# Sixteen partitions of the first five output-weight rows go in loads of 5, 5, 3 and 3 partitions

## The chip, the core and the metric

The kernel runs on one core of one Trainium2 chip. The metric is the time of one execution on the device, in microseconds (us). The times named "before" are of the kernel without the change.

## What is computed

A decode step with one new token for two batch rows. Half A is attention over a key and value cache of 16384 positions, 32 heads of 128; half B is a small mixer network; a gate adds them up.

```python
q = (x @ wq).reshape(B, Sq, H, Dh)                      # B=2, Sq=1, H=32, Dh=128, D=1024
scores = einsum("bhqd,bhkd->bhqk", q, k_cache) * Dh**-0.5
o = einsum("bhqk,bhkd->bhqd", softmax(scores), v_cache)
a = o.reshape(B, Sq, H * Dh) @ wo                       # wo: 4096 x 1024
b = x1 + gelu(layernorm(x1) @ w3) @ w4                  # x1 = x + shifted gelu(...) @ w2
out = g * a + (1 - g) * b                               # g = sigmoid(sum(x * gate_w))
```

The two caches are 537 MB of the 570 MB that the kernel reads. The output weights `wo` are 8 MB and are used last.

## The kernel before

All large loads are issued by SyncE (SP) into one ring of five slots in SBUF (`ring`), each of 32 KB in each of 128 partitions. A planner (`queue_load`, `pump`, `release`) keeps one list of loads in the order of use; a load is issued when its slots have been released by the matmuls that read them. First come `wq`, `w2`, `w3` and `w4`, then 32 rounds of a key load `k` and a value load `v` of 8 MB each, and at the end `wo` in two halves: ("wo", 0) into slot 2 and ("wo", 1) into slot 3.

Each partition holds 32 rows of `wo` (row r of partition p is row 32p + r of the matrix, 2 KB long). Half 0 is rows 0 to 15, and before the change it is one load of 128 partitions by 32 KB, made by the helper `runs` and issued on L335. Half 1 is rows 16 to 31; it comes in six pieces (`wo_runs[1]`) of 8, 4, 2, and then by columns 2, 1 and 1 rows, each with a semaphore of its own (`dtl0` to `dtl5`). The first three pieces are issued on L335, the last three, made by `cols_of`, on L341.

A round is: VectorE transposes blocks of the keys in place (L677), TensorE multiplies them by q (L683), a softmax follows (L693 to L710), TensorE multiplies by the values (L719), and the result goes to `OT_sb` (L728 to L733). After the last round `do_aproj` does the output projection: a transpose and a regrouping of `OT_sb` (L740 to L749), then for each row of `wo` four matmuls of 256 columns, each into its own quarter of the PSUM partitions (L766). Half 0 takes 64 of them, behind one wait. For half 1 the matmuls of the first two column quarters are on L766 (32 of them), and those of the other two are split into four of 128 columns per row (L778, 64 of them); each piece waits for its own semaphore. The chain ends with four copies out of PSUM (L804 to L808) and three stores (L806, L809).

Of the kernel before, what the change touches and what calls it, by code (L numbers as in the profile page):

```python
# [120 lines left out]
def build_kernel(nc, A_x, A_k, A_v, A_wq, A_wo, B_w1, B_w2, B_w3, B_w4, gate_w, out, dbg=None):  # L121
    dbg = dbg or {}
    B, Sq, D = A_x.shape
# [4 lines left out]
    P = 128  # L128
# [25 lines left out]
    RS = SLOT // D  # L154
# [6 lines left out]
               [(RS, RS // 2, *full), (RS + RS // 2, RS // 4, *full), (RO - RS // 4, RS // 8, *full),  # L161
                (RO - 2, 2, *lo), (RO - 2, 1, *hi_), (RO - 1, 1, *hi_)]]
    assert all(sum(n * qn for _, n, _, qn in runs) == RS * NQ for runs in wo_runs)
    DQ = D // NQ
    PR = 32 * (NQ - 1) + 2
    assert HQ == 2 and DQ <= 512 and HD == 8 * 512 and F % 8 == 0 and F <= 8 * 512 and P % (2 * NQ) == 0

    with ExitStack() as st:
# [3 lines left out]
        ring = sb("ring", [P, NRS, SLOT], BF16)  # L172
# [32 lines left out]
        OT4_sb = sb("OT4_sb", [P, RO, B], BF16)  # L205
        xrow = sb("xrow", [P, DQ], BF16)
        bgrow = sb("bgrow", [P, DQ], F32)
        orow = sb("orow", [P, DQ], BF16)
        lrow = sb("lrow", [2, 2 * DQ], BF16)
        m24 = sb("m24", [P, 2, NQ], F32)  # L210
# [21 lines left out]
        sem = lambda n: st.enter_context(nc.semaphore(n))  # L232
        esems = {e: sem("e_" + e) for e in ENGS}
        s_ring = [sem(f"dr{i}") for i in range(NRS)]
# [3 lines left out]
        s_out = [sem(f"dout{i}") for i in range(2)]  # L238
        s_fin = [sem(f"dfin{i}") for i in range(2)]
        s_xr = sem("dxr")  # L240
        s_tail = [sem(f"dtl{i}") for i in range(len(wo_runs[1]))]
        pl = _Plan(esems)

        def bank_bf(i):
            return banks[i].bitcast(BF16)
# [47 lines left out]
        dma_done = {}  # L293
# [13 lines left out]
        def pump():  # L307
            while dma_q and (dma_q[0][3] or all(i in slot_free for i in dma_q[0][2])):
                key, fns, slots, more = dma_q.pop(0)
                waits = () if more else sum((slot_free.pop(i) for i in slots), ())  # L310
                slot_of[key] = slots[0]
                slots_of[key] = slots
                for k, fn in enumerate(fns):
                    dsem = s_ring[slots[0]] if len(fns) == 1 else s_tail[k]
                    dyn = key[0] in ("k", "v") and key[1] >= B
                    if dyn and key == ("k", B):
                        pl.mark["sp"] = len(pl.ops["sp"])
                    one = (lambda e, i, fn=fn, idx=slots[0]: fn(e, idx, i)) if dyn else (lambda e, fn=fn, idx=slots[0]: fn(e, idx))
                    dma_done[key] = dma_done[key, k] = pl.dma("sp", one, dsem, waits=waits if k == 0 else (), dyn=dyn)

        def release(key, ev, slots=None):
            for idx in slots or slots_of[key]:
                assert idx not in slot_free
                slot_free[idx] = tuple(ev) if isinstance(ev, (tuple, list)) else (ev,)
            pump()
# [2 lines left out]
            assert key in dma_done, f"load {key} not yet issued in program order (would deadlock)"  # L328
            return dma_done[key]

        def runs(Wt, width, r0, rn, base=0):
            def fn(e, idx):
                src = Wt.rearrange("(p r) n -> p (r n)", p=P)[:, r0 * width:(r0 + rn) * width]
                flat = ring[:, idx:, :].rearrange("p s m -> p (s m)")
                return e.dma_start(flat[:, (r0 - base) * width:(r0 - base + rn) * width], src)  # L335
            return fn

        def cols_of(Wt, width, r0, rn, c0, cn, base):
            def fn(e, idx):
                dst = ring[:, idx, :].rearrange("p (r n) -> p r n", n=width)[:, r0 - base:r0 - base + rn, c0:c0 + cn]  # L340
                return e.dma_start(dst, Wt.rearrange("(p r) n -> p r n", p=P)[:, r0:r0 + rn, c0:c0 + cn])  # L341
            return fn

        wloads = {}
# [3 lines left out]
        for hi in range(2):  # L348
            wloads[("wo", hi)] = [runs(A_wo, D, r0, rn, hi * RS) if qn == NQ else cols_of(A_wo, D, r0, rn, q0 * DQ, qn * DQ, hi * RS)
                                  for r0, rn, q0, qn in wo_runs[hi]]  # L350
        wloads[("w2", 0)] = [runs(B_w2, D, 0, NBD)]

        w_slots = {"wq": (0, 1), "w2": (2,), "w3": (3, 4), "w4": (0, 1)}
# [27 lines left out]
        evd = {}  # L381
# [185 lines left out]
        key = ("w2", 0)  # L567
        put([row_stage(key, list(range(NBD)), 0, NBD, lambda kc: shT_bf[:, kc, :], "const", last=True), hs_columns], key)
        put([st_x1, ln_a(x1T_f[:, :, :], "x1", st2_ps, "xn2"), ln_b(st2_ps, "xn2", None)])
        key = ("w3", 0)  # L570
        put([w3_rows(kl) for kl in range(NBD)] + [w3_columns], key)
        put([gelu2])
        key = ("w4", 0)
# [16 lines left out]
        for pi in range(2):  # L590
            queue_load(("wo", pi), wloads[("wo", pi)], ((2, 3)[pi],))
        pump()

        def xcols(row, b_n, nb):
# [19 lines left out]
        key = ("wq", 0)  # L614
# [122 lines left out]
        def do_aproj():  # L737
            or_ps = bank_bf(7)[0:G, 256:256 + P]
            o4_ps = banks[3][:, 0:B * RO].rearrange("p (b r) -> p b r", b=B)
            e1 = pl.add("pe", lambda e: e.transpose(or_ps, OT_sb[:, :], ident[:, :]), waits=(ev_OT,), sig=True)  # L740
            e2 = pl.add("dve", lambda e: e.tensor_copy(OR_sb[:, :], or_ps), waits=(e1,), sig=True)  # L741
            ev = None
            for b in range(B):
                for dq in range(QO):
                    ev = pl.add("pe", lambda e, b=b, dq=dq: e.matmul(  # L745
                        o4_ps[:, b, :], lhsT=esel[:, b, :, dq], rhs=OR_sb[:, RO * dq:RO * (dq + 1)], start=(dq == 0), stop=(dq == QO - 1),
                        skip_group_check=True), waits=(e2, ev_const) if b + dq == 0 else (), sig=(b == B - 1 and dq == QO - 1))
            ev_half = [None, None]
            ev_o4 = pl.add("dve", lambda e: e.tensor_copy(OT4_sb[:, :, :].rearrange("p r b -> p b r"), o4_ps), waits=(ev,), sig=True)  # L749
            QC = DQ // 2  # L750
            ev_q2 = None
            for hi in range(2):
                key = ("wo", hi)
                wt = ring[:, slot_of[key], :].rearrange("p (r n) -> p r n", r=RS)
                for k, (r0, rn, q0, qn) in enumerate(wo_runs[hi]):
                    w = (dma_done[key, k], ev_o4, evd["bg"])
                    late = hi == 1
                    if late and ev_q2 is None:
                        for t in range(2):
                            ev_q2 = pl.add("dve", lambda e, t=t: e.tensor_copy(  # L760
                                q2_ps[64 * t:64 * t + 34, 0:QC], rows2_ps[64:98, QC * t:QC * (t + 1)]), waits=(ev_half[1],), sig=True)
                    wide = range(q0, min(q0 + qn, HQ) if late else q0 + qn)
                    for r in range(r0, r0 + rn):
                        for qd in wide:
                            ps = half(qd)
                            ev = pl.add("pe", lambda e, r=r, qd=qd, wt=wt, ps=ps: e.matmul(  # L766
                                ps[32 * qd:32 * qd + 2, 0:DQ], lhsT=OT4_sb[:, r, :], rhs=wt[:, r % RS, qd * DQ:(qd + 1) * DQ],
                                start=False, stop=True, tile_position=(0, 32 * qd), skip_group_check=True), waits=w,
                                sig=(qd == wide[-1]))
                            w = ()  # L770
                            ev_half[qd // HQ] = ev
                    if not late or q0 + qn == HQ:
                        continue
                    w = w + (ev_q2,)
                    for r in range(r0, r0 + rn):
                        for qd in range(NQ):
                            c = D // 2 + DQ * (qd % 2) + QC * (qd // 2)
                            ev_half[1] = pl.add("pe", lambda e, r=r, qd=qd, wt=wt, c=c: e.matmul(  # L778
                                q2_ps[32 * qd:32 * qd + 2, 0:QC], lhsT=OT4_sb[:, r, :], rhs=wt[:, r % RS, c:c + QC],
                                start=False, stop=True, tile_position=(0, 32 * qd), skip_group_check=True), waits=w,  # L780
                                sig=(qd == NQ - 1))
                            w = ()
            return ev_half
# [3 lines left out]
        for n in range(NPR):  # L787
# [3 lines left out]
            for k in range(0, NU, TC):  # L791
                ev_t = do_T(n, us[k])
                for t in range(TC):
                    w = () if t else (ev_t,) if k else (ev_t, ev_z) + pro_ev
# [51 lines left out]
def bass_gated_mix__mha_block_cached__mixer_s_mlp__decode_kernel(  # L846
    nc: bass.Bass,
    A_x: bass.AP,
    A_k_cache: bass.AP,
    A_v_cache: bass.AP,  # L850
    A_wq: bass.AP,
    A_wo: bass.AP,
    B_x: bass.AP,
    B_w1: bass.AP,
    B_w2: bass.AP,
    B_w3: bass.AP,
    B_w4: bass.AP,
    gate_w: bass.AP,
    out: bass.AP,
):  # L860
    build_kernel(nc, A_x, A_k_cache, A_v_cache, A_wq, A_wo, B_w1, B_w2, B_w3, B_w4, gate_w, out)
# [28 lines left out]
```

## Time and profile before

| what | value |
|---|---|
| median of 3 runs | 1324.05 us (1323.98 to 1324.16) |
| profiled execution, its time | 1324.2 us |
| profiled execution, span of its instructions | 1322.9 us |
| outside the span | 1.3 us |
| TensorE busy, VectorE busy | 59%, 50% of the span |
| read from HBM | 570.44 MB, 431 GB/s over the span |

The profile is of one execution, so sums are made against its 1324.2 us. It lies 0.15 us over the median of the runs shown. A time in the trace counts from the start of the span.

### The profile page before, as it was taken

How to read it: one execution, taken by the hardware profiler on the slowest of the kernel's cores; microseconds unless marked ns; L12 is line 12 of the kernel's file. 1: busy time of each engine (PE TensorE's matmuls, PEld its weight loads, DVE VectorE, ACT ScalarE, POOL GpSimd, SP SyncE). 2: the span in 40 equal slices, each digit the busy share in tenths (PEclk: the TensorE clock that was granted, in tenths of full speed). 3: DMA queues.
4: the chain of work that ended last, by engine and by line, in shares of the span. 5: the costliest groups of instructions: out<-in, count | busy, mean ns of one | idle time of the engine just before them, and what ended most of it. 6: DMA issues, size and time to landing. Idle time of an engine off the chain costs nothing. (4 is left out here: it accounts for less than half of the span.)

```text
span 1322.9 us, 12021 instructions
## 1 busy us (share of the span) xinstructions
PE 785.9 (59%) x4951; PEld 322.6 (24%) x4951; DVE 667.8 (50%) x541; ACT 46.4 (4%) x101; POOL 20.8 (2%) x96
## 2 busy tenths in 40 slices
PE   2345557655556765555676555567655556756557
PEld 1212222222222222222232222223222222322223
DVE  2264445655444665544466554446655445665444
ACT  0000000000000000000000000000000000000000
POOL 2000000000000000000000000000000000000000
PEclk9576788777678877767877776787777678777768
DMA  9999999999999999999999999999999999999998
GB/s 423 430 425 436 434 438 428 434 442 424 434 442 424 434 442 424 434 442 424 434 442 424 434 442 424 434 442 424 434 442 424 434 442 424 436 440 424 436 440 362
DMA packets 11114, 570.56 MB, mean 431 GB/s; under 512 B 1233, under 2 KB 1759, under 8 KB 1890
## 3 DMA queue, kind: packets, MB, share of 16 engines
q1 hardware_dynamic: 11080, 570.43, 99.7%
q8 instruction: 6, 0.10, 0.0%
q10 hardware_dynamic: 26, 0.01, 0.0%
q14 instruction: 2, 0.02, 0.0%
HBM read 570.44 MB, written 0.00 MB: 431 GB/s over the span
## 5 line engine op out<-in xcount | busy, mean ns | idle before, releaser
L683 PE MATMUL ps<-ring,Z 128*128 128x512 bf16 x2048 | 533.2, 418 | 377.3 <-DVE ring L677 376.3
L677 DVE STREAM_TRANSPOSE ring<-ring 128x2048 f32<-128x2048 f32 x256 | 565.2, 2275 | 264.8 <-DMA ring<-in_A_k_cache_dram 264.8
L683 PEld LDWEIGHTS ps<-ring,Z 128*128 128x128 bf16 x2048 | 203.4, 104 | 694.4 <-issue 457.1
L719 PE MATMUL ps<-ring,PT_sb 128*32 128x512 bf16 x2048 | 178.8, 526 | 4.3 <-DVE recip L710 3.9
L733 DVE SCALAR_TENSOR_TENSOR OT_sb<-ps,gT,recip 128x2 f32 x32 | 7.0, 220 | 214.3 <-PE ps L730 214.3
L719 PEld LDWEIGHTS ps<-ring,PT_sb 128*32 128x32 bf16 x2048 | 69.8, 127 | 99.4 <-issue 83.4
L704 ACT ACTIVATE P_sb<-ps,negm 128x512 bf16<-128x512 f32 x32 | 22.0, 687 | 1000.0 <-DVE negm L702 1000.0
L693 DVE TENSOR_REDUCE rA<-ps 128x1 f32<-128x512 f32 x32 | 22.1, 692 | 64.2 <-PE ps L683 64.2
L708 PE MATMUL ps<-rowsum,hsel 128*128 128x1 f32 x128 | 24.2, 293 | 38.0 <-ACT P_sb L704 38.0
L706 DVE STREAM_TRANSPOSE PT_sb<-P_sb 128x512 bf16<-128x512 bf16 x32 | 22.8, 712 | 27.1 <-ACT P_sb L704 27.1
L708 PEld LDWEIGHTS ps<-rowsum,hsel 128*128 128x128 f32 x128 | 21.5, 238 | 40.7 <-ACT P_sb L704 40.7
L663 POOL TENSOR_TENSOR Z<-q_f,mask 128x8 bf16<-128x8 f32 x64 | 12.3, 228 | 1210.2 <-PE ps L683 1210.2
L695 PE MATMUL ps<-ident,rmax_bf 128*1 128x128 bf16 x32 | 6.9, 217 | 33.1 <-DVE rmax_bf L694 33.1
L728 ACT ACTIVATE acc_sb<-ps 128x512 bf16<-128x512 f32 x32 | 19.1, 597 | 209.8 <-PE ps L719 209.8
L730 PE MATMUL ps<-dsel,acc_sb 128*128 128x2 bf16 x128 | 8.1, 167 | 22.6 <-ACT acc_sb L728 22.6
L621 PE MATMUL ps<-ring,xT_bf 128*2 128x512 bf16 x64 | 5.2, 494 | 16.4 <-DMA ring<-in_A_wq_dram 16.4
L730 PEld LDWEIGHTS ps<-dsel,acc_sb 128*128 128x128 bf16 x128 | 5.3, 96 | 38.3 <-ACT acc_sb L728 38.3
L695 PEld LDWEIGHTS ps<-ident,rmax_bf 128*1 128x1 bf16 x32 | 2.5, 79 | 48.9 <-DVE rmax_bf L694 48.9
L696 DVE TENSOR_REDUCE m_sb<-ps 1x2 bf16<-1x128 bf16 x32 | 8.9, 279 | 9.9 <-PE ps L695 9.9
L702 DVE TENSOR_SCALAR negm<-ps,cAB 128x1 f32<-128x1 f32 x32 | 8.9, 278 | 9.2 <-PE ps L699 9.2
L699 PE MATMUL ps<-m_sb,ones_bf 1*64 1x1 bf16 x64 | 6.1, 186 | 11.9 <-DVE m_sb L696 11.9
L520 PE MATMUL ps<-ring,GT_bf 128*2 128x256 bf16 x112 | 5.2, 372 | 6.8 <-DMA ring<-in_B_w_dram 6.8
(113 smaller groups left out, 93.6 us busy)
## 6 DMA issues: line engine op xcount, KB each, us to landing
ring<-in_B_w_dram SPq DMA_DIRECT2D x2, 7168.0 KB, 39.1
ring<-in_A_wq_dram SPq DMA_DIRECT2D x1, 7168.0 KB, 21.3
ring<-in_A_wo_dram SPq DMA_DIRECT2D x1, 4096.0 KB, 37.5
ring<-in_B_w_dram SPq DMA_DIRECT2D x1, 2048.0 KB, 25.5
ring<-in_A_wo_dram SPq DMA_DIRECT2D x1, 2048.0 KB, 22.1
ring<-in_A_wq_dram SPq DMA_DIRECT2D x1, 1024.0 KB, 4.6
ring<-in_A_wo_dram SPq DMA_DIRECT2D x1, 1024.0 KB, 24.3
ring<-in_A_k_cache_dram SPq DMA_DIRECT2D x32, 26.7
```

Of the source, the lines that this page charges most:

```text
L663: return e.tensor_tensor(Z[:, :, ZO:ZO + P].rearrange("p t (i c) -> p t i c", c=32)[:, :, 2 * hp:2 * hp + 2, hp], q4_f[:, :, col].broadcas ...
L677: return pl.add("dve", lambda e: e.transpose(ap, ap), waits=(arrived(("k", n)),), sig=True)
L683: ev = pl.add("pe", lambda e, bp=bp: e.matmul(S_ps[:, 0:NCOL], lhsT=Z[:, bp, ZO - 2 * u:ZO - 2 * u + P], rhs=kv[:, :, bp // 2, :, bp % 2], ...
L693: e1 = pl.add("dve", lambda e: e.tensor_reduce(rA[:, :], S_ps[:, 0:NCOL], axis=AX.X, op=ALU.max), waits=(ev_S[n],), sig=True)
L695: e3 = pl.add("pe", lambda e: e.transpose(mt_ps, rmax_bf[:, :], ident[:, :]), waits=(e2,), sig=True)
L696: e4 = pl.add("dve", lambda e: e.tensor_reduce(m_sb[0:1, :], mt_ps.rearrange("o (h p) -> o h p", h=HP), axis=AX.X, op=ALU.max), waits=(e3, ...
L704: e7 = pl.add("act", lambda e: e.activation(P_sb[:, :], S_ps[:, 0:NCOL], ACT.Exp, bias=negm[:, 0:1], scale=scale, accum_out=rowsum[:, 0:1] ...
L706: e8 = pl.add("dve", lambda e: e.transpose(PT_sb[:, :], P_sb[:, :]), waits=(e7,), sig=True)
L708: e9 = pl.add("pe", lambda e, hp=hp: e.matmul(l_ps[:, hp:hp + 1], lhsT=hsel[:, hp, :], rhs=rowsum[:, 0:1], start=True, stop=True, skip_gro ...
L719: ev = pl.add("pe", lambda e, jj=jj, cg=cg: e.matmul(acc_ps[32 * cg:32 * cg + 32, 0:512], lhsT=PT_sb[:, 32 * jj:32 * jj + 32], rhs=vv[:, 4 ...
L728: e1 = pl.add("act", lambda e: e.activation(acc_sb[:, :], acc_ps[:, 0:512], ACT.Copy), waits=(ev_pv,), sig=True)
L730: e2 = pl.add("pe", lambda e, w=w: e.matmul(oT_ps, lhsT=acc_sb[:, w * P:(w + 1) * P], rhs=dsel[:, w, :], start=(w == 0), stop=(w == 3)), w ...
```

## The change

Half 0 of `wo`, rows 0 to 15, is no longer one load. Rows 0 to 4 of partitions 0 to 111 are one load, rows 5 to 15 of all 128 partitions are a second, and rows 0 to 4 of partitions 112 to 127 come in four more loads of 5, 5, 3 and 3 partitions. The bytes are the same and they land in the same places. The first two loads have a semaphore each (`dw0`, `dw1`), the four short ones share the third (`dw2`). All six are issued where the one was, and all wait for the same slot. The first matmul of half 0 waits for all three semaphores.

```diff
+    ER = 5
+    e_parts = (5, 5, 3, 3)
+    EP = P - sum(e_parts)
...
+        s_w0 = [sem(f"dw{i}") for i in range(3)]
...
-                    dsem = s_ring[slots[0]] if len(fns) == 1 else s_tail[k]
+                    dsem = s_ring[slots[0]] if len(fns) == 1 else s_w0[min(k, 2)] if key == ("wo", 0) else s_tail[k]
...
-        def runs(Wt, width, r0, rn, base=0):
+        def runs(Wt, width, r0, rn, base=0, p0=0, pn=P):
             def fn(e, idx):
-                src = Wt.rearrange("(p r) n -> p (r n)", p=P)[:, r0 * width:(r0 + rn) * width]
-                flat = ring[:, idx:, :].rearrange("p s m -> p (s m)")
+                src = Wt.rearrange("(p r) n -> p (r n)", p=P)[p0:p0 + pn, r0 * width:(r0 + rn) * width]
+                flat = ring[p0:p0 + pn, idx:, :].rearrange("p s m -> p (s m)")
...
+        wloads[("wo", 0)] = [runs(A_wo, D, 0, ER, 0, 0, EP), runs(A_wo, D, ER, RS - ER, 0)]
+        wloads[("wo", 0)] += [runs(A_wo, D, 0, ER, 0, EP + sum(e_parts[:j]), k) for j, k in enumerate(e_parts)]
...
-                    w = (dma_done[key, k], ev_o4, evd["bg"])
+                    w = (dma_done[key, k], ev_o4, evd["bg"]) + ((dma_done[key, 1], dma_done[key, 1 + len(e_parts)]) if hi == 0 else ())
```

On SP, behind the loop over the rounds, this is what stood after the last value load (partitions by elements of 2 bytes):

```order
L100 COMPARE_AND_BRANCH
L335 DMA ring<-in_A_wo_dram 128x16384
L335 DMA ring<-in_A_wo_dram 128x8192 [waits e_pe]
L335 DMA ring<-in_A_wo_dram 128x4096
L335 DMA ring<-in_A_wo_dram 128x2048
```

And this is what stands there now:

```order
L100 COMPARE_AND_BRANCH
L340 DMA ring<-in_A_wo_dram 112x5120
L340 DMA ring<-in_A_wo_dram 128x11264
L340 DMA ring<-in_A_wo_dram 5x5120 x2
L340 DMA ring<-in_A_wo_dram 3x5120 x2
L340 DMA ring<-in_A_wo_dram 128x8192 [waits e_pe]
L340 DMA ring<-in_A_wo_dram 128x4096
```

One load has become six, all ahead of the wait for slot 3 that half 1 has; nothing behind that wait moved.

On TensorE, at the start of the output projection, before the change (`dr2` is the semaphore of ring slot 2, `e_dve` that of VectorE's work):

```order
L745 MATMUL ps<-OR_sb,esel 128x32 [waits e_pool,e_dve]
L745 MATMUL ps<-OR_sb,esel 128x32 x7
L766 MATMUL ps<-ring,OT_sb 2x256 [waits e_dve,dr2]
L766 MATMUL ps<-ring,OT_sb 2x256 x63
L766 MATMUL ps<-ring,OT_sb 2x256 [waits dtl0]
```

And with it:

```order
L752 MATMUL ps<-OR_sb,esel 128x32 [waits e_pool,e_dve]
L752 MATMUL ps<-OR_sb,esel 128x32 x7
L773 MATMUL ps<-ring,OT_sb 2x256 [waits dw1,dw2,e_dve,dw0]
L773 MATMUL ps<-ring,OT_sb 2x256 x63
L773 MATMUL ps<-ring,OT_sb 2x256 [waits dtl0]
```

The wait for one load has become three, two of which stand ahead of the wait for VectorE; the matmuls and their order are the same.

## Rows read from the trace of the kernel before

**Rows 1.** The page: DMA busy in 40 slices, moved GB/s, queues with their packets
```profile
DMA  9999999999999999999999999999999999999998
GB/s 423 430 425 436 434 438 428 434 442 424 434 442 424 434 442 424 434 442 424 434 442 424 434 442 424 434 442 424 434 442 424 434 442 424 436 440 424 436 440 362
...
q1 hardware_dynamic: 11080, 570.43, 99.7%
q8 instruction: 6, 0.10, 0.0%
q10 hardware_dynamic: 26, 0.01, 0.0%
q14 instruction: 2, 0.02, 0.0%
HBM read 570.44 MB, written 0.00 MB: 431 GB/s over the span
```

**Rows 2.** The chain that ended last: start us, us, what
```profile
1313.16 0.24 DVE OT_sb L749
1313.41 0.14 issue
1313.54 4.71 PE ps L766 x65
...
1320.64 0.17 PE ps L766 x2
1320.81 0.02 issue
1320.83 0.38 ACT lrow L805
1321.20 0.02 issue
1321.23 0.27 ACT orow L808
```

**Rows 3.** Timeline of the output projection: start us, us, engine, line, what, count
```profile
1312.41 0.22 DVE L741 COPY OR_sb<-ps 64x128 bf16<-64x128 bf16 x1 [0.58 <-PE ps L740]
1312.68 0.44 PE L745 MATMUL ps<-OR_sb,esel 64*128 64x32 bf16 x8 [0.31 <-DVE OR_sb L741]
1313.16 0.23 DVE L749 CAST OT_sb<-ps 128x64 bf16<-128x64 f32 x1 [0.54 <-PE ps L745]
1313.54 4.86 PE L766 MATMUL ps<-ring,OT_sb 128*2 128x256 bf16 x76 [0.42 <-DVE OT_sb L749]
1318.41 1.17 PE L778 MATMUL ps<-ring,OT_sb 128*2 128x128 bf16 x28
1320.62 0.34 PE L778 MATMUL ps<-ring,OT_sb 128*2 128x128 bf16 x6
```

**Rows 4.** Stretches: busy us of PE, PEld, DVE, ACT, POOL; PEclk; DMA share; GB/s
```profile
1310.00:1318.00 8.00, 5.78 (x99) 3.48 (x93) 1.28 (x5) 0.60 (x1) 0.00 (x0) 0.66 0.98 404
1318.00:1318.50 0.50, 0.50 (x14) 0.34 (x12) 0.00 (x0) 0.00 (x0) 0.00 (x0) 0.50 1.07 373
1318.50:1319.00 0.50, 0.50 (x22) 0.42 (x18) 0.00 (x0) 0.00 (x0) 0.00 (x0) 0.50 0.88 268
1319.00:1319.25 0.25, 0.25 (x17) 0.25 (x10) 0.00 (x0) 0.00 (x0) 0.00 (x0) 0.50 0.47 164
1319.25:1319.50 0.25, 0.25 (x12) 0.25 (x8) 0.00 (x0) 0.00 (x0) 0.00 (x0) 0.81 0.46 160
1319.50:1319.75 0.25, 0.25 (x17) 0.19 (x11) 0.00 (x0) 0.00 (x0) 0.00 (x0) 1.00 0.35 123
1319.75:1320.00 0.25, 0.25 (x19) 0.23 (x12) 0.00 (x0) 0.00 (x0) 0.00 (x0) 1.00 0.32 111
1320.00:1320.25 0.25, 0.25 (x20) 0.23 (x12) 0.00 (x0) 0.00 (x0) 0.00 (x0) 1.00 0.19 66
1320.25:1320.50 0.25, 0.25 (x14) 0.22 (x10) 0.00 (x0) 0.00 (x0) 0.00 (x0) 1.00 0.00 0
```

**Rows 5.** Line L341, the last three loads: issue ns, first and last start; landing
```profile
L341 SPq DMA_DIRECT2D ring<-in_A_wo_dram x3: 432/434/467, 1294.8 to 1295.8; - x3
...
DMA to landing us min/median/max: 24.9/25.1/25.2
```

**Rows 6.** DMA issues of the page: count, KB each, us from issue to landing
```profile
ring<-in_A_wo_dram SPq DMA_DIRECT2D x1, 4096.0 KB, 37.5
...
ring<-in_A_wq_dram SPq DMA_DIRECT2D x1, 1024.0 KB, 4.6
```

**Rows 7.** Line L335 from 1272 us on, the other four loads of wo
```profile
L335 SPq DMA_DIRECT2D ring<-in_A_wo_dram x4: 338/386/434, 1273.2 to 1294.3; - x4
```

**Rows 8.** What SP's queue waited for: us in total, times, longest us
```profile
SPq L335 <- PE ps L683: 19.9, 1, 19.9
```

**Rows 9.** Line L778: ns min/median/max of its matmuls, first and last start
```profile
L778 PE MATMUL ps<-ring,OT_sb x64: 217/220/314, 1318.0 to 1320.7; 128*2 128x128 bf16 x64
```

More of the change, by code (lines that the diff above doesn't have):

```diff
@@ L163, in build_kernel @@
     assert all(sum(n * qn for _, n, _, qn in runs) == RS * NQ for runs in wo_runs)
+    ER = 5
+    e_parts = (5, 5, 3, 3)
+    EP = P - sum(e_parts)
+    assert EP % 16 == 0 and ER < RS
     DQ = D // NQ
```

## The prediction

> **What bounds the kernel now.** First the page's slices [rows 1]: the DMA queues are busy in every slice at 424 to 442 GB/s, and only the last falls to 362. For 1310 of 1323 us the kernel is as fast as its bytes come in. The change moves the same bytes, so nothing can be won or lost there by a better rate; what is open is the end, where the bytes run out.
>
> Second the chain that ended last [rows 2]: the projection's matmuls start at 1313.54, when VectorE's cast of 1313.16 is done, and run without a gap to 1320.81, where the copies out begin. [...]
>
> Third the DMA's own end. The share of the 16 queues that work is about full to 1318.5, 0.88 in the half microsecond up to 1319.0, then 0.47, 0.46, 0.35, 0.32, 0.19 in quarters, and 0 from 1320.25 on [rows 4]. So some eight or nine queues are done at about 1319.0 and the rest finish over the next 1.2 us: the queues got equal bytes and don't end together. The last of the loads, issued at 1295.8, lands 24.9 us later, at 1320.7 [rows 5]. The four matmuls that need it are the last four on L778; the group of six that begins at 1320.62 ends at 1320.96, and one takes 0.22, so the last start is at 1320.74 [rows 3, 9]. **Both ends meet within 0.1 us:** the matmuls reach the last piece at about 1320.7, and it lands at 1320.7.
>
> How a load is shared among the queues can be counted. On q1, SP issued 76 loads of 128 partitions and two stores of two rows. One packet per row (two per row for the one piece that takes two rows by columns) is 77 x 128 + 4 = 9860, with 16 completions per load 1216 more, with two per store 4 more: 11080, the number of the row [rows 1]. On q10, ScalarE's queue, seven small transfers with 13 rows in all have 26 packets [rows 1]: 13 rows and 13 completions. So a load of 128 partitions runs on 16 queues with eight rows each, and a transfer of two rows on two.
>
> **What the change does to each queue.** A queue moves 431 / 16 = 26.9 GB/s, so five rows of one partition, 10,240 bytes, are 10.24 / 26.9 = 0.38 us. The load of 112 partitions has seven such pieces per queue in place of eight: 0.38 us less on all 16. The 16 pieces left over go to the short loads. If a load of five uses five queues and one of three uses three, as two rows use two, and each load begins at the same first queue, three queues get four pieces (net +3, 1.14 us more), two queues get two (net +1, 0.38 us more) and eleven get 0.38 us less. That is a levelling where the loaded queues are among the early ones. The early ones end at about 1319.0 and would end at 1319.0 + 1.14 = 1320.15; the late ones end at 1320.25 and would end at 1319.87. The last landing then moves by -0.1 us, and by -0.38 us if the early queues end a little sooner than the windows can tell. No view names the queues, so that the loaded ones are early is a choice; the other case is a rival. If the short loads took turns over the queues instead, each queue would get one piece back, and the last landing would stay where it is; the time would be the same as in the forecast.
>
> [...]
>
> **What that is worth at the end.** Only the last four matmuls wait for the last landing, and TensorE gets there by its own work 0 to 0.1 us earlier. So of an earlier landing 0 to 0.1 us comes through; I take 0.05, since the landing at 1320.7 and the start at 1320.74 differ by less than the rounding. After that the matmuls, which have no gap from 1313.54 on, are what is late.
>
> **What it adds.** On SP five more loads, at 0.39 us each [rows 7] 1.9 us, all ahead of a wait of 19.9 us for the slot of half 1 [rows 8]: nothing, as long as that wait is there, and 1.9 us on each later load if it were gone. Behind them stand only the six pieces of half 1, which keep their release. On TensorE two more waits before the first matmul of half 0. Half 0 landed at 1273.2 + 37.5 = 1310.7 [rows 6, 7], and the matmul starts at 1313.54, so 2.8 us of slack cover a landing that is 1.14 us later. The price of the wait instructions themselves: from the end of the cast (1313.39) to the matmul are 0.15 us with two waits, and at L745, also two waits, from 1312.63 to 1312.68 0.05 us [rows 3]. One extra wait can thus cost up to 0.1 us, or nothing where it runs while TensorE waits for the cast, 0.42 us [rows 3]. The two extra ones stand ahead of the wait for VectorE in the built order, so I take 0 and keep 0.1 for the range. Packets: half 0 has 256 rows in place of 128 and up to 16 + 16 + 16 completions in place of 16, 160 more on 11,080; the mean rate can't show that.
>
> **Sum.** TensorE 0 (0 to +0.1), end -0.05 (-0.1 to 0): -0.05 us on 1324.2, or 1324.0 against the median of 1324.05, which is 0.15 under the profiled execution.
>
> **The rivals.**
>
> (1) *The landing sets the end after all.* The starts and ends of matmuls are partly modelled, and TensorE's clock was at its low level for most of the tail; an execution that gets the high level earlier has the matmuls waiting for each piece. Then the whole -0.1 to -0.38 us comes through: 1323.7. For it: the landing and the last start coincide. Against it: no idle time and no wait on a load from 1313.54 on [rows 2, 4].
>
> (2) *The loaded queues are among the late ones.* Then a queue that ended at 1320.25 ends up to 1.14 us later (three queues), or 0.38 (two queues), and the last four matmuls wait for it: +0.4 to +1.1 us, 1324.45 to 1325.2. For it: at 0.47 of 16 some seven queues are still at work after 1319.0 [rows 4], and nothing in the views says that the first five are not among them. Against it: nothing either; it gets less than the forecast because even with one of the two-piece queues late the loss is 0.4 us and hard to see.
>
> (3) *A short load does not spread.* A load of five or three rows runs on one queue, and all four on the same. That queue gets 16 pieces in place of one: 15 x 0.38 = 5.7 us more. If it was early (1319.0), its last landing comes 4.5 us after the others' old end, near 1325.2; if late, near 1326.4. End: +4.5 to +5.7, 1328.5 to 1329.7, slower by 0.34 to 0.43%. It decides from the point where one queue gets more than 1.2 us. For it: no load of five or three rows stands in the trace. Against it: two-row transfers did use two queues [rows 1].
>
> (4) *A short load pays a fixed price and holds its queue.* The smallest load with nothing ahead of it took 4.6 us for 1024 KB, 2.4 of them at 431 GB/s, so 2.2 us are fixed [rows 6]. Four of those in a row are 8.8 us: half 0 lands at 1319.5, 6 us after it is wanted, and the end moves to about 1330. Against it: the three loads of L341, issued at 1294.8 to 1295.8, land 24.9 to 25.2 us after their issue, so they follow each other by half a microsecond and the fixed part overlaps [rows 5]. [...]
>
> **How the numbers follow.** A measurement of this kernel tells about 0.2% from no change, 2.6 us. The forecast, 1324.0 with TensorE at the end, gets 0.70; the landing at the end, 1323.7, 0.09; late queues loaded, 1324.45 to 1325.2, 0.16; one queue for all 0.03; a fixed price each 0.01; a gain of over 2.6 us, for which I have no mechanism, 0.01. The range reaches from the first rival's lower end, 1323.65, less the 0.1 us by which the runs shown differ, to the second's upper, 1325.2; it leaves out 5 in 100, and two steps of the sum (which queues are late, what of it comes through) are bounded from both sides by it. Within 0.2%: 0.70 + 0.09 + 0.16 = 0.95. Slower by over 0.2%: 0.04. Faster: 0.01.
>
> **What would show it.** Right: the projection's first matmul starts within 0.1 us of where it did, no idle time on TensorE up to the copies, and the DMA share of the last windows is steeper, with more in 1319.0 to 1319.75 and nothing after about 1320.2. The last three loads land about 0.1 to 0.4 us earlier after their issue. Rival 2 shows as a landing of over 25.3 us and a gap before the last matmuls; rival 3 as a DMA share of 0.06, one queue of 16, for several microseconds; rival 4 as a wait of the first matmul on a load of `wo`. A changed rate in the slices of the loop would make the whole reading wrong, since the change does not touch the loop.

## The result, and the profile after

The changed kernel takes 1330.89 us (median of six runs, 1330.68 to 1331.14), the kernel before on the same chip 1324.07 us (1323.95 to 1324.28). The ratio is 1.0051, with a 95% interval of 1.0041 to 1.0062: **6.82 us slower**, where -0.05 us was forecast and 1325.2 us was the upper end of the range. The execution profiled after took 1331.14 us with a span of 1329.8, so 6.9 us of span are to be found against the 1322.9 before.

The page first, the lines that answer to [rows 1]:

```profile
DMA  9999999999999999999999999999999999999998
GB/s 424 425 438 420 439 434 440 424 438 434 440 422 438 436 438 424 436 438 438 424 432 440 440 424 432 440 440 424 432 440 436 428 432 440 432 432 432 440 430 277
...
q1 hardware_dynamic: 11240, 570.43, 99.7%
...
HBM read 570.44 MB, written 0.00 MB: 429 GB/s over the span
```

Up to the last slice the loop moves its bytes as before, at 420 to 440 GB/s. The last slice falls to 277, from 362. The bytes of q1 are the same, its packets are 160 more.

The stretches of the end, kernel after (start:end, length, busy us of PE, PEld, DVE, ACT, POOL with their instructions, granted clock, DMA share, GB/s; PE is TensorE, PEld its weight loads, DVE is VectorE, ACT ScalarE, POOL GpSimd):

```profile
1300.00:1304.00 4.00, 1.92 (x10) 0.66 (x8) 1.47 (x4) 0.32 (x1) 0.00 (x0) 1.00 1.05 227
1304.00:1308.00 4.00, 3.27 (x56) 1.94 (x60) 0.83 (x2) 0.46 (x2) 0.00 (x0) 1.00 0.92 266
1308.00:1312.00 4.00, 1.88 (x33) 0.88 (x25) 0.67 (x3) 0.60 (x1) 0.00 (x0) 1.00 1.00 414
1312.00:1317.00 5.00, 0.00 (x0) 0.00 (x0) 0.00 (x0) 0.00 (x0) 0.00 (x0) 0.66 0.97 208
1317.00:1320.00 3.00, 2.42 (x48) 1.60 (x52) 0.00 (x0) 0.00 (x0) 0.00 (x0) 0.50 1.00 423
```

The same stretches of the kernel before:

```profile
1300.00:1304.00 4.00, 1.68 (x9) 0.57 (x7) 1.46 (x4) 0.56 (x1) 0.00 (x0) 1.00 1.12 483
1304.00:1308.00 4.00, 3.52 (x40) 1.84 (x44) 0.83 (x2) 0.22 (x2) 0.00 (x0) 0.71 0.99 426
1308.00:1312.00 4.00, 2.67 (x40) 1.07 (x32) 0.22 (x1) 0.60 (x1) 0.00 (x0) 0.86 0.91 389
1312.00:1317.00 5.00, 4.12 (x75) 2.73 (x77) 0.45 (x2) 0.00 (x0) 0.00 (x0) 0.55 0.97 405
```

Two columns matter. The DMA share, second from the right, is near 1 in both kernels: the queues are busy all the time. What they deliver, the last column, falls to about half in two stretches of the changed kernel, 1300 to 1308 (227 and 266 GB/s after 483 and 426) and 1312 to 1317 (208 after 405). From 1300 to 1317 the kernel before moves 4 x (483 + 426 + 389) + 5 x 405 = 7217 KB and the one after 4 x (227 + 266 + 414) + 5 x 208 = 4668 KB. The missing 2549 KB are 5.9 us at 431 GB/s; the last microsecond of the 6.9 lies behind 1317, where the queues end further apart than before (below), or in the edges of the windows.

What that does to TensorE, the timeline of the kernel after around the projection (start us, us, engine, line, what, count, idle time before it and what ended it), answering to [rows 3], and its waits (total us, times, longest):

```profile
1311.72 0.23 DVE L756 CAST OT_sb<-ps 128x64 bf16<-128x64 f32 x1 [0.53 <-PE ps L752]
...
1317.58 3.30 PE L773 MATMUL ps<-ring,OT_sb 128*2 128x256 bf16 x64 [5.90 <-DMA ring<-in_A_wo_dram]
...
1322.83 0.82 PE L773 MATMUL ps<-ring,OT_sb 128*2 128x256 bf16 x12 [1.95 <-DMA ring<-in_A_wo_dram]
...
1325.38 0.38 PE L773 MATMUL ps<-ring,OT_sb 128*2 128x256 bf16 x4 [1.06 <-DMA ring<-in_A_wo_dram]
...
1327.59 0.54 PE L785 MATMUL ps<-ring,OT_sb 128*2 128x128 bf16 x8
```

```profile
PE ps L773 <- DMA ring<-in_A_wo_dram: 9.3, 4, 5.9
```

The cast is done at 1311.95, and the first matmul of half 0 starts at 1317.58: it waits 5.90 us for a load of `wo`. The 2.8 us by which half 0 was early before are used up and more. From there on TensorE follows the landings. In [rows 2] the chain that ended last runs through the projection's matmuls; now the long row near its end (start us, us, what) is a load that is issued at 1297.34 and lands at 1327.85, with four matmuls and a copy behind it:

```profile
1297.34 30.51 DMA ring<-in_A_wo_dram
```

The landings of half 0 and the wait of SP's queue, kernel after, answering to [rows 6 to 8]:

```profile
ring<-in_A_wo_dram SPq DMA_DIRECT2D x1, 2816.0 KB, 42.6
...
ring<-in_A_wo_dram SPq DMA_DIRECT2D x1, 1120.0 KB, 34.1
```

```profile
SPq L340 <- PE ps L690: 18.1, 1, 18.1
```

The load of 112 partitions (1120 KB), issued at 1273.9, lands at 1308.0, where the first slow stretch ends. Behind it the 2816 KB of 128 partitions come in at the full rate at first (414 GB/s from 1308 to 1312). But this load, issued at 1274.3, lands only at 1316.9, at the end of the second slow stretch, in which the short loads move too; in the first run below, which has no short loads, it is issued at 1272.7 and lands 38.1 us later, at 1310.8. SP's wait fell by 1.8 us, which is what the five added issues take: they are hidden, as expected.

### The profile page after: what moved, and what is told of

It is laid out like the page before. It is cut to its first block, busy times and chain, and to the rows that moved or that the text cites. A ratio compares the mean times of both kernels' runs of the same rounds, so it can differ in the third digit from the quotient of the medians.

```text
span 1329.8 us, 12027 instructions
## 1 busy us (share of the span) xinstructions
PE 776.1 (58%) x4951; PEld 319.7 (24%) x4951; DVE 667.9 (50%) x541; ACT 46.4 (3%) x101; POOL 20.8 (2%) x96
## 4 chain that ended last, share of the span: by engine, by line
DMA 70%; PE 23%; DVE 6%; issue 1%; SPq 0%
DMA ring<-in_A_k_cache_dram 65%; PE ps L690 22%; DVE ring L684 6%; DMA ring<-in_B_w_dram 3%; DMA ring<-in_A_wo_dram 2%; PE ps L483 0%; SPq L340 0%; SPq L370 0%; SPq L346 0%; DVE orow L814 0%; PE ps L785 0%
## 5 line engine op out<-in xcount | busy, mean ns | idle before, releaser
L726 PE MATMUL ps<-ring,PT_sb 128*32 128x512 bf16 x2048 | 168.3, 502 | 4.1 <-DVE recip L717 3.7
L773 PE MATMUL ps<-ring,OT_sb 128*2 128x256 bf16 x96 | 5.7, 353 | 9.5 <-DMA ring<-in_A_wo_dram 9.3
```

Of the source, the lines that this page charges most:

```text
L726: ev = pl.add("pe", lambda e, jj=jj, cg=cg: e.matmul(acc_ps[32 * cg:32 * cg + 32, 0:512], lhsT=PT_sb[:, 32 * jj:32 * jj + 32], rhs=vv[:, 4 ...
```

## The experiments

Each kernel ran once, beside one run of the kernel before on the same chip. The six runs of the result spread by 0.33 us (before) and 0.46 us (after), so a difference of less than half a microsecond tells little by itself. Diffs are against the changed kernel and show the changed lines only; in all but the second run the waits of the first matmul of half 0 are fitted to its loads, and these lines are left out. The theories that the expectations name:

- **P**: the partitions that a load writes set its rate: a load of all 128 goes at the full rate, one of 112 or of neighbouring rows does not, and rows four apart cost their bytes alone.
- **S**: pieces of 10 KB, 64 KB apart in HBM, are read slowly.
- **Q**: the short loads overload a few queues, and nothing else matters.
- **N**: a load of few partitions is slow in itself.
- **B**: only the bytes on the most loaded queues count. **T**: a passing loss when loads of another kind come along.

**1. The rows split, the partitions not.** Rows 0 to 4 and 5 to 15 are a load of 128 partitions each; there are no short loads.

```diff
-        wloads[("wo", 0)] = [runs(A_wo, D, 0, ER, 0, 0, EP), runs(A_wo, D, ER, RS - ER, 0)]
-        wloads[("wo", 0)] += [runs(A_wo, D, 0, ER, 0, EP + sum(e_parts[:j]), k) for j, k in enumerate(e_parts)]
+        wloads[("wo", 0)] = [runs(A_wo, D, 0, ER, 0), runs(A_wo, D, ER, RS - ER, 0)]
```

> Half 0 of the output weights in two loads of all 128 partitions, rows 0 to 4 and rows 5 to 15; no load of 112 partitions and no short loads. [...] Theory S (pieces of 10 KB that lie 64 KB apart in HBM are read at half the rate, whatever partitions they go to): 207 GB/s for some 6 us as in the changed kernel, about 3.4 us lost, end 3 us later than before.

1324.07 against 1324.12 us: the loss is gone. The stretches of this kernel, columns as above:

```profile
1300.00:1304.00 4.00, 1.64 (x9) 0.56 (x7) 1.46 (x4) 0.60 (x2) 0.00 (x0) 1.00 1.07 452
1304.00:1308.00 4.00, 3.55 (x32) 1.65 (x36) 0.83 (x2) 0.18 (x2) 0.00 (x0) 0.61 1.03 439
```

The same 10-KB pieces at the same places in HBM move at 452 and 439 GB/s. S falls: what counts is which partitions a load covers.

**2. One short load in place of four.**

```diff
-    e_parts = (5, 5, 3, 3)
+    e_parts = (16,)
```

> As the changed kernel, but rows 0 to 4 of partitions 112 to 127 come in one load of 16 partitions, one row per queue, in place of loads of 5, 5, 3 and 3. [...] Theory Q (the short loads of fewer than 16 partitions are what costs, through a few queues that carry them all): close to the kernel before, at most 1 us over it. Theory S: 3.4 us over the kernel before.

1329.61 against 1324.12: +5.49 us, where Q gave at most 1 and S 3.4. With one load of 16 partitions (281 and 263 GB/s at a DMA share of 1.05 from 1312 to 1314 and 1314 to 1316) most of the 6.82 us is still there, so a pile on a few queues isn't the bulk of it.

**3. The load of 112 partitions alone.** The short loads are left out.

```diff
-        wloads[("wo", 0)] += [runs(A_wo, D, 0, ER, 0, EP + sum(e_parts[:j]), k) for j, k in enumerate(e_parts)]
```

> The first load of 112 partitions and the second of 128, without any load for rows 0 to 4 of partitions 112 to 127: these 160 KB are left out, so the result lacks their part. The price of the 112 partitions alone. Theory P: 207 GB/s or so while the first load runs, 3 to 3.5 us over the kernel before. Theory Q: as the kernel before within 0.4 us.

1327.26 against 1324.12: +3.14 us with 0.38 us of bytes fewer, so the rate lost 3.52 us.

```profile
1300.00:1304.00 4.00, 1.84 (x10) 0.63 (x8) 1.46 (x4) 0.40 (x1) 0.00 (x0) 1.00 1.01 228
1304.00:1308.00 4.00, 3.35 (x44) 1.88 (x48) 0.83 (x2) 0.38 (x2) 0.00 (x0) 0.82 0.96 295
1308.00:1312.00 4.00, 2.83 (x35) 1.03 (x24) 0.22 (x1) 0.60 (x1) 0.00 (x0) 0.75 1.00 426
1312.00:1317.00 5.00, 3.56 (x69) 2.39 (x73) 0.45 (x2) 0.00 (x0) 0.00 (x0) 0.66 0.98 416
```

The first slow stretch is there, the second is gone. From 1300 to 1317 this makes 5876 KB, 1341 fewer than before, 3.1 us at 431 GB/s: most of these 3.52 us. Q falls, since there is no short load here; the packets of q1 are 11208, which is 112 rows and 16 completions more than before and fits a load over all 16 queues.

**4. The same, with another source.** The 112 partitions read consecutive addresses, in the key cache; the write side is that of the third run.

```diff
+        def packed(e, idx):
+            src = A_k[0, 0, 0:EP * ER * D // Dh, :].rearrange("(p j) d -> p (j d)", p=EP)
+            return e.dma_start(ring[0:EP, idx, 0:ER * D], src)
+
-        wloads[("wo", 0)] = [runs(A_wo, D, 0, ER, 0, 0, EP), runs(A_wo, D, ER, RS - ER, 0)]
-        wloads[("wo", 0)] += [runs(A_wo, D, 0, ER, 0, EP + sum(e_parts[:j]), k) for j, k in enumerate(e_parts)]
+        wloads[("wo", 0)] = [packed, runs(A_wo, D, ER, RS - ER, 0)]
```

> As the run with the 112 partitions alone, but its rows of 10 KB are read from consecutive addresses of the key cache, so the result is not the projection's; the partitions written are the same 112. Theory P (the write side): as slow as the run with the 112 partitions alone, 3 to 3.5 us over the kernel before. Theory S (the read side): back at the kernel before within 0.4 us.

1327.58 against 1324.12: +3.46 us. The slow stretch is there again, at 222 and 269 GB/s:

```profile
1300.00:1304.00 4.00, 1.75 (x10) 0.56 (x7) 1.47 (x4) 0.48 (x1) 0.00 (x0) 1.00 1.04 222
1304.00:1308.00 4.00, 3.44 (x40) 1.81 (x44) 0.83 (x2) 0.29 (x2) 0.00 (x0) 0.76 0.93 269
```

The side that is written decides, not the side that is read; the 0.3 us between this run and the third is no more than runs of one kernel differ.

**5 to 8. Sixteen rows more, put into different partitions.** The kernel is that of the first run, with 16 rows of `wo` (160 KB, 0.38 us at 431 GB/s) loaded once more, into a tile that nothing reads; half 0 waits for them too. Only the partitions and the split change. The edit, on top of the first run's:

```diff
+        scratch = sb("scratch", [P, 5120], BF16)
...
+        def extra(p0, pn, st):
+            def fn(e, idx):
+                src = A_wo.rearrange("(p r) n -> p (r n)", p=P)[112:112 + pn, 0:ER * D]
+                return e.dma_start(scratch[p0:p0 + (pn - 1) * st + 1:st, :], src)
+            return fn
...
+        wloads[("wo", 0)] += [extra(*x) for x in [(112, 16, 1)]]
```

The list holds (first partition, rows, step). The sixth, seventh and eighth run have in its place:

```diff
-        wloads[("wo", 0)] += [extra(*x) for x in [(112, 16, 1)]]
+        wloads[("wo", 0)] += [extra(*x) for x in [(0, 16, 8)]]
...
+        wloads[("wo", 0)] += [extra(*x) for x in [(112, 5, 1), (117, 5, 1), (122, 3, 1), (125, 3, 1)]]
...
+        wloads[("wo", 0)] += [extra(*x) for x in [(0, 5, 4), (1, 5, 4), (2, 3, 4), (3, 3, 4)]]
```

> Half 0 in two loads of 128 partitions, which alone cost nothing, and behind them one extra load of 16 rows of 10 KB into partitions 112 to 127 of a tile that nothing reads (160 KB more than the kernel before, 0.38 us at the mean rate). [...]

> The same extra load of 16 rows, but into partitions 0, 8, 16 and so on to 120 of the unused tile. [...] Theory N: as the run with the 16 neighbours, 2 to 2.7 us over.

> Half 0 in two loads of 128 partitions, and behind them four extra loads of 5, 5, 3 and 3 rows of 10 KB into partitions 112 to 127 of the unused tile. The changed kernel was 3.6 us over the run that lacks its short loads. Theory P: 3.5 to 4.5 us over the kernel before. Theory B (only the bytes on the three most loaded queues count, 4 x 0.38 us, less what these queues were early): 0.3 to 1.5 us over.

> The same four extra loads of 5, 5, 3 and 3 rows, but into partitions four apart (0, 4, 8, 12, 16; 1, 5, 9, 13, 17; 2, 6, 10; 3, 7, 11) of the unused tile, so that the rows of one load lie in different groups of four. Theory P: what is left is the bytes, 0.3 to 1.5 us over the kernel before. Theory N (loads of few partitions are slow in themselves): as the run before this one, 3.5 to 4.5 us over.

All against 1324.23 us: the fifth 1326.41, +2.18; the sixth 1325.69, +1.46, under the 2 to 2.7 that N gave it; the seventh 1327.84, +3.61; the eighth 1324.83, +0.60. The seventh and the eighth are the pair to look at: the same bytes in the same loads of 5, 5, 3 and 3 rows with the same number of packets on q1 (11256), only the partitions differ, and one costs 3.0 us more. Their rates in the stretch where the extra rows move, seventh run first:

```profile
1309.00:1313.00 4.00, 2.82 (x40) 0.97 (x29) 0.22 (x1) 0.60 (x1) 0.00 (x0) 0.81 0.99 171
```

```profile
1309.00:1313.00 4.00, 1.83 (x52) 1.45 (x53) 0.67 (x3) 0.60 (x1) 0.00 (x0) 1.00 0.99 420
```

At the same DMA share of 0.99, 171 GB/s against 420. N falls: a load of three or five partitions is not slow in itself. The fifth run has 252 GB/s there.

```profile
1309.00:1313.00 4.00, 2.98 (x40) 1.09 (x32) 0.07 (x1) 0.60 (x1) 0.00 (x0) 0.78 0.93 252
```

Together with the third run this adds up to the change: 3.14 for the 112 partitions and 3.61 for the short loads are 6.75 us, of 6.82 measured (the 0.38 us of bytes that the third run lacks are the seventh's extra ones). For the second run 3.14 and 2.18 are 5.32, of 5.49.

**9 and 10. Sixteen rows in one load, four apart and seven apart.** In the ninth run the extra rows go into partitions 32, 36 and so on to 92, in the tenth into 11, 18 and so on to 116. The edit is against the fifth run.

```diff
-        wloads[("wo", 0)] += [extra(*x) for x in [(112, 16, 1)]]
+        wloads[("wo", 0)] += [extra(*x) for x in [(32, 16, 4)]]
...
+        wloads[("wo", 0)] += [extra(*x) for x in [(11, 16, 7)]]
```

> [...] Theory P: only the bytes, 0.2 to 0.6 us over the kernel before (160 KB at 431 GB/s are 0.38 us). If a load of 16 partitions cost something of its own, it would be over 1 us.

> [...]

1324.64 and 1325.37 against 1324.17: +0.47, which the bytes (0.38) explain within the spread of runs, and +1.20, 0.8 us more than the bytes. From 1309 to 1313 the ninth run moves 430 GB/s at a DMA share of 1.01, the tenth 337 at 0.97.

**11 and 12. The same four times over.** Here the extra rows are 655 KB, 1.52 us at 431 GB/s; in the eleventh run they go into partitions 32 to 95, each load into every fourth, in the twelfth into every seventh from 11, 3, 7 and 19. The edit is against the fifth run again.

```diff
-        wloads[("wo", 0)] += [extra(*x) for x in [(112, 16, 1)]]
+        wloads[("wo", 0)] += [extra(*x) for x in [(32, 16, 4), (33, 16, 4), (34, 16, 4), (35, 16, 4)]]
...
+        wloads[("wo", 0)] += [extra(*x) for x in [(11, 16, 7), (3, 16, 7), (7, 16, 7), (19, 16, 7)]]
```

> [...] Theory P: the bytes alone, 655 KB at 431 GB/s, 1.5 to 1.7 us over the kernel before. If each load of 16 partitions had a price of its own, four times what the one had over its bytes (0.09 us), at most 0.4 us more.

> [...] Theory T (the loss is a passing one of about 0.8 us per change of the pattern, whatever the number of rows): 2.3 to 2.5 us over.

1325.95 and 1328.12 against 1324.44: +1.51, the bytes, and +3.68, 2.2 us more than the bytes. The rates, eleventh run first:

```profile
1309.00:1313.00 4.00, 2.20 (x30) 0.86 (x22) 0.44 (x2) 0.60 (x1) 0.00 (x0) 0.91 1.01 427
```

```profile
1309.00:1313.00 4.00, 2.19 (x42) 0.95 (x31) 0.44 (x2) 0.60 (x1) 0.00 (x0) 1.00 1.04 249
```

427 against 249 GB/s at a full DMA share. B falls by the seventh run, for which it gave 0.3 to 1.5 us, and the twelfth. T falls too: a passing loss would have left the tenth run's 0.8 us over the bytes, and it grew to 2.2 with four times the rows. The loads are four times as many as well, so a loss for each row and one for each such load are not told apart.

## Why the prediction was wrong

**The step that failed** is a sentence of the first part: "The change moves the same bytes, so nothing can be won or lost there by a better rate". That bytes bound the kernel was right, and the loop's slices are as they were; but the rate was taken as given. On that rest the 0.38 us per row for every load, and the term for the packets at nothing. The rate of 26.9 GB/s per queue was read from loads of 128 partitions, all that [rows 1] has of any size, and carried to loads of 112, 5 and 3. In its place the runs show a rate that hangs on the partitions that are written: 222 to 295 GB/s over all queues while the 112 move, 171 to 252 with 16 rows into partitions 112 to 127 (seventh and fifth run), and 420 to 427 where the rows go four apart (eighth and eleventh). In the sum this is +3.1 to +3.5 us for the load of 112 partitions (third and fourth run) and +3.6 us for the short loads (seventh), where -0.38 and a levelling stood.

**What covers were worth.** Half 0 had 2.8 us of slack, rightly read; a term of 1.14 us fitted into it. The true terms did not, and they cost in full in any case: the late bytes of half 0 push those of half 1 behind them, so the last landing moves by all that the queues lose (1327.85 after, 1320.7 before). Slack of the first matmul could have hidden a late half 0, but not a lost rate. The seventh run has it so: the first matmul of half 0 follows VectorE's cast there (a pause of 0.37 us) and waits for no load, and the end is 3.61 us later all the same.

**Which end decides.** The forecast put TensorE at the end, rival 1 the landing, and both had them within 0.1 us. The first run decides for the landing: there TensorE's granted clock is 1.00 from 1312 to 1317, where before it was 0.55, and TensorE has pauses before the pieces and ends at the same time all the same. Its stretch and its last pause for a piece:

```profile
1312.00:1317.00 5.00, 3.90 (x121) 2.98 (x121) 1.06 (x4) 0.00 (x0) 0.00 (x0) 1.00 0.98 407
```

```profile
1319.50 0.27 PE L772 MATMUL ps<-ring,OT_sb 128*2 128x256 bf16 x2 [0.51 <-DMA ring<-in_A_wo_dram]
```

So 1.00 in place of 0.55 bought nothing: "TensorE 0" held, for the reason that the rival gave.

**Counting the packets** held. The 160 more on q1 are 128 rows, 16 completions of the second large load, 5 + 5 + 3 + 3 of the short ones. So the short loads did spread, on five and three queues, and rival 3, one queue for all, falls. Its 1328.5 to 1329.7 is on the side and near the size of the result, by another mechanism. Rival 4, a fixed price for each short load, names 1330 and falls by the eighth run, where the four cost 0.60 us together. The sign that it was to show by, a wait of the first matmul on a load of `wo`, is there, and would have misled a reader who stopped at it.

**That the loaded queues are early ones** is a choice that the eighth run speaks for: if the loads pile up as the prediction has it, three queues get four pieces more, 1.52 us, and the end moves by 0.60, so these had some 0.9 us to spare. If they take turns, each queue gets 0.38 us, and the 0.60 says nothing about early queues. That every short load begins at the same first queue, on which the -0.1 us of the last landing rests, no run shows; what the runs show of four such loads is the +3.61 us of the seventh and the +0.60 of the eighth. **The levelling** itself did not come. The end of the kernel after, columns as above:

```profile
1319.50:1325.00 5.50, 2.86 (x80) 1.86 (x72) 0.61 (x2) 0.00 (x0) 0.00 (x0) 0.91 0.97 390
1325.00:1326.00 1.00, 0.62 (x24) 0.54 (x24) 0.00 (x0) 0.00 (x0) 0.00 (x0) 1.00 0.75 258
1326.00:1327.00 1.00, 0.58 (x22) 0.30 (x14) 0.00 (x0) 0.00 (x0) 0.00 (x0) 1.00 0.15 51
1327.00:1328.00 1.00, 0.79 (x17) 0.27 (x12) 0.34 (x1) 0.34 (x1) 0.00 (x0) 1.00 0.03 9
```

Before, the queues ended within 1.2 us, from 1319.0 to 1320.25 [rows 4]; now the share needs 2 to 3 us to go from full to nothing, and 0.15 and 0.03 are of two or three queues and of less than one. **SP's five issues** cost nothing, as said, and no price of **the two more waits** shows, since the first matmul waits for its loads. What the prediction did not have is that the last three issues now take 6.61 us in place of 1.42:

```profile
1295.47 6.61 SPq L346 DMA_DIRECT2D ring<-in_A_wo_dram  x3
```

This is not where the time goes: the same three take 4.3 us in the first run and 6.9 in the eleventh, and these lose nothing beyond their bytes.

**What could have been known.** [Rows 1 to 9] hold loads of 128 partitions and transfers of one or two rows, and no other shape. So the price of a load of 112 had to be bounded from both sides, and the prediction set it at the full rate without an end on the slower side. Its 2.6 us for what a measurement tells from no change is also far wider than the 0.33 and 0.46 us by which six runs of one kernel spread. The runs show what the range left out: rows in loads of 16, four apart, cost their bytes (ninth and eleventh run: 0.47 and 1.51 us, against 0.38 and 1.52), the same bytes put elsewhere 2.4 times that (twelfth run) to 9.5 times (seventh).

**What stays open.** By which mechanism the written partitions set the rate. No view shows which queue carries which row, so the runs tell only which partitions were written fast and which slowly. That the load of 112 partitions is slow, and that its source is not the reason, is shown (third and fourth run: +3.14 and +3.46 us), but no run has a load of 112 rows on other partitions. Nor is it shown what spares the rows of the eighth, ninth and eleventh run: they lie four apart, but all from a start in partitions 0 to 3 or 32 to 35, and a run with rows four apart from another start is missing. And of the 3.6 us of the short loads the bytes explain 0.38; the same 16 rows in one load cost 2.18 (fifth run), and why four loads cost 1.4 us more was not found: see the last section.

## What to carry to other kernels

A load that fills all 16 queues is not yet a load at full rate (227 GB/s at a DMA share of 1.05 in the kernel after): look at GB/s beside the DMA share, and keep loads of a bandwidth-bound kernel at 128 partitions, cut along the free dimension, which cost nothing here (-0.05 us). If rows have to be taken out for single partitions, spread them four apart as in the eighth and ninth run; the same 160 KB cost 0.47 us so against 2.18 us as a block of neighbours in one load, and 0.60 against 3.61 us in four loads. Where the profile holds one shape only, its rate is no bound for another: a range has to have an end for that.

## What was not expected of the hardware

A few rows slow every queue. In the short loads' stretch all 16 are busy at a share of 0.97 and move 208 GB/s, though by the packets a load of five rows ran on five queues and one of three on three. The load of 128 partitions that was issued ahead of them is late too: its 2816 KB land at 1313.5 in the seventh run, and at 1311.0 in the eighth, with the same short loads on other partitions (1310.8 in the first, which has none). Were only these queues held up, the others would be done well before the end (an estimate: some 3 us, the loss that the short loads brought), and the share would drop ahead of it; it is 0.97 up to 1325.0. By which mechanism the others are held up, the runs do not tell.

A step of four partitions within a load costs no rate by itself: the eleventh run moves 427 GB/s with it, and the twelfth, with a step of seven, 249. The slow stretches also do not look like idle time anywhere on the profile's page: its slices of DMA show 9, 9 and 8 in the last three, as before the change, and only GB/s tells.
